# A dynamic convolution with a maxout layer: first chunk in halves with a bit mask for its halo, weights doubled by ScalarE, softmax one chunk ahead of the sums, output copies of two PSUM banks

## The chip, the cores and the metric

The kernel runs on one core of one Trainium2 chip. Times are device microseconds (us) of one execution. "Span" is the time from the first to the last instruction of the profiled execution; it is 1.7 to 2.2 us shorter than the time of that same execution.

## The reference

A causal convolution over 7 rows whose weights are different at each row and for each of 8 groups of 24 columns (a softmax of 7 given numbers), then a layer that takes the larger of two products and projects back.

```python
# x (8, 4160, 192), weight_gen (8, 4160, 8, 7), moe_w1, moe_w2 (192, 1024), moe_w_out (1024, 192)
w = np.exp(weight_gen - max); w = w / (sum(w) + 1e-9)          # over the 7
x_pad = concatenate([zeros(B, 6, D), x], axis=1)               # the halo of each sequence is zero
y[b, s, h, g] = sum over k of w[b, s, h, k] * x_pad[b, s + k, h, g]
h1 = y @ w1; h2 = y @ w2
out = np.maximum(h1, h2) @ w_out
```

## The kernel before

Partition p holds 260 consecutive rows, so 16 partitions hold one sequence. The rows are taken in "chunks" (8, 8, 8, then 14 of 16, then 8 and 4 rows a partition), each chunk in "units" of 8 rows (4 in the first two and the last). VectorE makes the softmax and the convolution of a chunk; a DMA transposes it to `yt`; TensorE makes the hidden layer of a unit while it makes the outputs of the unit before; ScalarE does exp, relu and the output copies. max(h1, h2) is computed as h1 + relu(h2 - h1), so only the difference `wd` of the weights goes through the hidden layer and a small product `w10` gives the first term.

The convolution multiplies 24 columns by one weight. Each weight is stored twice (`[1, 2]`, innermost), so that the multiply reads the weights in pairs. The product e x 1/sum writes both copies itself:

```python
def conv(ci):                                   # VectorE, one chunk; TH = rows * 8 heads, n = rows * 192
    nc.vector.reduce_sum(out=sum_t, in_=_sub(e_t, 0, [[K, TH], [1, K]]), axis=AX.X)
    nc.vector.reciprocal(out=rec_t, in_=sum_t)
    nc.vector.tensor_tensor(                    # "the product": bf16, each weight written twice
        out=_sub(en_t, 0, [[2, TH], [2 * TH, K], [1, 2]]),
        in0=_sub(e_t, 0, [[K, TH], [1, K], [0, 2]]),
        in1=_sub(rec_t, 0, [[1, TH], [0, K], [0, 2]]), op=ALU.mult)
    nc.vector.tensor_tensor(out=m_t, in0=..., in1=..., op=ALU.mult)    # "the multiply": 7 shifted rows of x
    if ci + 2 < len(CHUNKS):
        load(ci + 2)
    # ... three adds, the last into y_t
```

```python
# start: the zero halo of each sequence's first partition is a transfer of its own,
# ahead of the five weight transfers in the same queue
nc.sync.dma_start(out=xb_t[0:P:RPB, 0:PAD * D], in_=zero_t[0:P:RPB, :])
# ... exp(0); conv(0); weight subtractions on VectorE; weight casts on ScalarE; w10 by TensorE
for u in range(NU + 1):
    while queued < NCH and queued <= UNITS[min(u + 3, NU - 1)][0]:
        exp(queued); conv(queued); queued += 1  # exp(1) comes after all weight casts on ScalarE
    if u == 0: transpose(0)
    if u + 1 < NU: transpose(u + 1)             # ahead of unit u's output transfer in the queue
    # ... four quarters: hidden matmuls, relus, output matmuls, one copy of 384 elements per output pair
```

The softmax here doesn't subtract the row's maximum and nothing guards it: scores larger than these inputs give would overflow.

## Time and profile before

| | before |
|---|---|
| time, median of 3 runs | 477.84 us |
| span of the profiled run | 476.3 us |
| TensorE / VectorE / ScalarE busy | 90% / 88% / 71% |
| start of the fifth unit on TensorE | 88.41 us |
| VectorE, one 16-row chunk | 25.6 us |
| TensorE, two units | 25.24 us |

Two views are added. The first is the summary of the chain of waits, which is followed back from the last instruction; it gives each engine's share of the span.

```profile
PE 81%; DVE 11%; DMA 5%; SPq 1%; ACT 1%; issue 0%; POOLq 0%
```

TensorE carries four fifths of it: after the start, TensorE works and the rest keeps up. The second view is VectorE's timeline over one chunk in mid-kernel (start us, duration us, instruction, output<-inputs).

```profile
191.05 11.36 DVE L138 TENSOR_TENSOR m_t<-xb_t,en_t 128x21504 bf16<-128x21504 bf16 x1
...
214.61 2.03 DVE L130 TENSOR_TENSOR en_t<-e_t,rec_t 128x1792 bf16<-128x1792 bf16 x1
216.67 11.36 DVE L138 TENSOR_TENSOR m_t<-xb_t,en_t 128x21504 bf16<-128x21504 bf16 x1
```

From one multiply to the next are 25.62 us, with no gap. VectorE is thus within 0.4 us of TensorE's 25.24: a chunk may grow by nothing on VectorE without the bound moving there.

### The profile page before, as it was taken

To read this page: it belongs to the slowest core of one execution; us is meant where nothing else is said; L and a number is where in the kernel's file an instruction comes from. 1 tells how busy PE (TensorE), PEld (TensorE's weight loads), DVE (VectorE), ACT (ScalarE), POOL (GpSimd) and SP (SyncE) were. 2 spreads that over 40 slices of the span, in tenths; PEclk is the share of its full clock that TensorE was granted. 3 is DMA by queue.
4 is the path that set the end of the run, shared out by engine and by line. 5 is a ranking of instruction groups with operands and counts; after the bars stand their busy time and mean duration, and the time that the engine had idled before them with its cause. 6 is when DMAs were issued, how large, how long until landed. Compare 5 with 4: busy or idle time off the path is not lost.

```text
span 476.3 us, 8155 instructions
## 1 busy us (share of the span) xinstructions
PE 427.1 (90%) x3606; PEld 271.5 (57%) x3606; DVE 418.6 (88%) x136; ACT 336.5 (71%) x437; POOL 22.1 (5%) x46
## 2 busy tenths in 40 slices
PE   0087695599999999999999999989999999999997
PEld 0054353366666666666666666656666666666675
DVE  2949999999999999999999999999999999997000
ACT  1266374287877878787878787867878787777773
POOL 3000000000000000000000000000000000000000
PEclk9999698599999999999999999999999999999999
DMA  8945745546574737467585747384736537273212
GB/s 168 261 107 104 170 120 129 133 93 169 131 175 123 199 107 174 150 139 190 131 200 125 206 85 219 76 192 109 200 109 139 172 67 200 43 200 100 83 67 100
DMA packets 62131, 67.47 MB, mean 142 GB/s; under 512 B 52329, under 2 KB 53609, under 8 KB 60304
## 3 DMA queue, kind: packets, MB, share of 16 engines
q1 hardware_dynamic: 57792, 41.12, 31.1%
q0 software_dynamic: 4304, 25.84, 24.9%
q8 instruction: 28, 0.46, 0.4%
q14 instruction: 7, 0.06, 0.0%
HBM read 46.58 MB, written 25.56 MB: 151 GB/s over the span
## 4 chain that ended last, share of the span: by engine, by line
PE 81%; DVE 11%; DMA 5%; SPq 1%; ACT 1%; issue 0%; POOLq 0%
PE op_ps L292 34%; PE hdp L243 22%; PE hdp L258 13%; PE op_ps L279 7%; DVE m_t L138 5%; PE op_ps L287 4%; DMA wso<-in_moe_w_out_dram 3%; DVE m_t L149 2%; DMA yt<-y_t 2%; DVE m_t L151 1%; DVE en_t L130 1%; PE pw L211 1%; DVE y_t L154 1%; DMA wg_t<-in_weight_gen_dram 1%; DVE sum_t L125 1%; DVE rec_t L127 1%
## 5 line engine op out<-in xcount | busy, mean ns | idle before, releaser
L269 ACT ACTIVATE rd_t<-hdp 128x1024 bf16<-128x1024 f32 (+1 forms) x272 | 267.5, 986 | 112.0 <-PE hdp L258 77.2
L292 PE MATMUL op_ps<-wo,rd_t 128*128 128x192 bf16 x2080 | 216.6, 248 | 0.0
L292 PEld LDWEIGHTS <-rd_t 128*128 128x128 bf16 x2080 | 177.8, 99 | 23.7 <-issue 0.9
L138 DVE TENSOR_TENSOR m_t<-xb_t,en_t 128x21504 bf16<-128x21504 bf16 (+2 forms) x19 | 185.0, 9738 | 5.5 <-DMA xb_t<-zero_t 4.9
L243 PE MATMUL hdp<-yt,wdE 128*128 128x512 bf16 (+1 forms) x272 | 101.6, 374 | 20.8 <-DMA yt<-y_t 18.3
L243 PE MATMUL hdp<-yt,wdO 128*128 128x512 bf16 (+1 forms) x272 | 101.5, 373 | 0.0
L258 PE MATMUL hdp<-yt,wdR 64*128 64x512 bf16 (+1 forms) x544 | 81.6, 375 | 1.1 <-ACT rd_t L269 1.1
L149 DVE TENSOR_TENSOR m_t<-m_t 128x9216 bf16<-128x9216 bf16 (+2 forms) x19 | 81.0, 4263 | 0.7
L303 ACT COPY o_t<-op_ps 128x384 f32<-128x384 f32 x130 | 61.6, 474 | 2.5 <-PE op_ps L292 2.3
L151 DVE TENSOR_TENSOR m_t<-m_t 128x6144 bf16<-128x6144 bf16 (+2 forms) x19 | 55.0, 2894 | 0.7
L258 PEld LDWEIGHTS <-wdR 64*128 64x128 bf16 x544 | 16.2, 94 | 58.1 <-issue 57.5
L279 PE MATMUL op_ps<-w10R,yt 128*128 128x384 bf16 x130 | 44.0, 339 | 0.0
L279 PEld LDWEIGHTS <-yt 128*128 128x128 bf16 x130 | 12.4, 96 | 53.1 <-issue 52.8
L243 PEld LDWEIGHTS <-wdE 128*128 128x128 bf16 x272 | 26.8, 99 | 22.0 <-DMA yt<-y_t 19.6
L287 PEld LDWEIGHTS <-yt 128*128 128x128 bf16 x260 | 25.7, 99 | 14.8 <-issue 0.6
L130 DVE TENSOR_TENSOR en_t<-e_t,rec_t 128x1792 bf16<-128x1792 bf16 (+2 forms) x19 | 33.4, 1755 | 0.7
L287 PE MATMUL op_ps<-w10E,yt 128*128 128x192 bf16 x130 | 32.2, 248 | 0.0
L287 PE MATMUL op_ps<-w10O,yt 128*128 128x192 bf16 x130 | 32.2, 248 | 0.0
L154 DVE TENSOR_TENSOR y_t<-m_t 128x3072 bf16<-128x3072 bf16 (+2 forms) x19 | 29.0, 1527 | 0.7
L243 PEld LDWEIGHTS <-wdO 128*128 128x128 bf16 x272 | 26.8, 99 | 3.6 <-issue 3.4
L125 DVE TENSOR_REDUCE sum_t<-e_t 128x128 f32<-128x896 bf16 (+2 forms) x19 | 17.9, 944 | 9.9 <-ACT e_t L115 9.9
L105 POOL DMA_DIRECT2D xb_t<-in_x_dram x18 | 9.5, 529 | 333.4 <-DVE m_t L138 333.4
(29 smaller groups left out, 69.0 us busy)
## 6 DMA issues: line engine op xcount, KB each, us to landing
out_dram<-o_t SPq DMA_DIRECT2D x31, 768.0 KB, 3.9
xb_t<-in_x_dram POOLq DMA_DIRECT2D x14, 1056.0 KB, 7.8
wg_t<-in_weight_gen_dram POOLq DMA_DIRECT2D x14, 448.0 KB, 6.1
xb_t<-in_x_dram POOLq DMA_DIRECT2D x3, 672.0 KB, 7.9
wg_t<-in_weight_gen_dram POOLq DMA_DIRECT2D x4, 224.0 KB, 5.5
wso<-in_moe_w_out_dram SPq DMA_DIRECT2D x1, 768.0 KB, 13.5
out_dram<-o_t SPq DMA_DIRECT2D x2, 384.0 KB, 3.6
yt<-y_t SPq DMA_TRANSPOSE x34, 3.8
```

Source lines behind the costliest of these rows:

```text
L130: nc.vector.tensor_tensor(out=_sub(en_t, 0, [[2, TH], [2 * TH, K], [1, 2]]), in0=_sub(e_t, 0, [[K, TH], [1, K], [0, 2]]), in1=_sub(rec_t, ...
L138: nc.vector.tensor_tensor(out=m_t, in0=_sub(xb_t, 0, [[D, K], [1, n]]), in1=_sub(en_t, 0, [[2 * TH, K], [2, TH], [0, D // H // 2], [1, 2]] ...
L149: nc.vector.tensor_tensor(out=m_t[:, 0:3 * n], in0=m_t[:, 0:3 * n], in1=m_t[:, 3 * n:6 * n], op=ALU.add)
L151: nc.vector.tensor_tensor(out=rows(m_t, 2, 2, 0), in0=rows(m_t, 2, 2, 0), in1=rows(m_t, 5, 2, 1), op=ALU.add)
L154: nc.vector.tensor_tensor(out=y_t, in0=m_t[:, 0:n], in1=m_t[:, 2 * n:3 * n], op=ALU.add)
L243: nc.tensor.matmul(hd_ts[u, f][:, j * 512:j * 512 + N], lhsT=wd[kind][:, f * P:(f + 1) * P], rhs=_sub(yt_ts[u], 2 * j * P, [[3 * P, n // 2 ...
L258: nc.tensor.matmul(hd_ts[u, f][:, j * 512:j * 512 + N], lhsT=wd["R"][r, f * P:(f + 1) * P], rhs=_sub(yt_ts[u][r, :], P, [[3 * P, n // 2], ...
L269: nc.scalar.activation(out=_sub(rd_ts[u], f * 1024, [[512, 2], [1, N]]), in_=_sub(hd_ts.pop((u, f)), 0, [[512, 2], [1, N]]), func=AF.Relu,)
L279: nc.tensor.matmul(op[:, 0:2 * D], lhsT=yt[:, (3 * i + 1) * P:(3 * i + 2) * P], rhs=w10R, start=True, stop=False, skip_group_check=True,)
L287: nc.tensor.matmul(op[:, sl], lhsT=yt[:, (3 * i + 2 * j) * P:(3 * i + 2 * j + 1) * P], rhs=(w10E, w10O)[j], start=False, stop=False, skip_ ...
L292: nc.tensor.matmul(op[:, sl], lhsT=rd[:, f, j * 512 + i * P:j * 512 + (i + 1) * P], rhs=wo[:, f * D:(f + 1) * D], start=False, stop=(f == ...
L303: nc.scalar.copy(out=o_ts[u][:, 2 * i * D:2 * (i + 1) * D], in_=op_ts.pop((u, i))[:, 0:2 * D])
```

## The change

Its intent: get the first chunk to TensorE sooner (no zero transfer, chunk 0 in two halves), take half the product off VectorE by writing single weights and letting ScalarE double them, put the softmax of the next chunk between a chunk's multiply and its sums so that neither ScalarE nor VectorE waits for it, move the weight subtractions to GpSimd, and copy outputs two banks at a time. The core of the diff:

```diff
+    DIRECT = 2                                   # chunks 0 and 1 are still doubled by VectorE
-            nc.sync.dma_start(out=xb_t[0:P:RPB, 0:PAD * D], in_=zero_t[0:P:RPB, :])
+            halo = xb_t[:, 0:PAD * D].bitcast(I32)
+            nc.vector.tensor_scalar(out=halo, in0=halo, scalar1=msk[:, 0:1], scalar2=None,
+                                    op0=ALU.bitwise_and)
 ... soft(ci): reduce, reciprocal, then
+        pair = 2 if ci < DIRECT else 1
+        for o, To in pieces(ci):                 # two halves in chunk 0, else the chunk
+            N = To * H
 ...
+                en_t = pe_.tile([P, K * N], BF16, name="e1_t", tag="e1")
+            nc.vector.tensor_tensor(
+                out=_sub(en_t, 0, [[pair, N], [pair * N, K], [1, pair]]),
+                in0=_sub(e_t, o * WGC, [[K, N], [1, K], [0, pair]]),
+                in1=_sub(rec_t, o * H, [[1, N], [0, K], [0, pair]]),
+                op=ALU.mult,
+            )
+    def dup(ci):
 ...
+        nc.scalar.copy(out=_sub(en_t, 0, [[2, KTH], [1, 2]]),
+                       in_=_sub(e1_ts.pop(ci), 0, [[1, KTH], [0, 2]]))
 ... start
+        exp(1)
+        for o in (0, 4):
+            mul(0, o)
+            adds(0, o)
+        load(2)
-            nc.vector.tensor_tensor(out=dst, in0=ws[kind, 1], in1=ws[kind, 0], op=ALU.subtract)
+            nc.gpsimd.tensor_tensor(out=dst, in0=ws[kind, 1], in1=ws[kind, 0], op=ALU.subtract)
+        soft(1)
+        mul(1)
+        load(3)
 ... w10R is still cleared by GpSimd further down, now behind load(3)
 ... in the loop over units, ca = the next chunk when unit u ends one
+                if i == 1:
+                    if ca + 1 < NCH:
+                        dup(ca + 1)
+                    adds(ca)
+                    if ca + 1 < NCH:
+                        mul(ca + 1)
+                    if ca + 3 < NCH:
+                        load(ca + 3)
+                if i == 2 and ca + 2 < NCH:
+                    exp(ca + 2)
+                    soft(ca + 2)
+            if i == 3 and u + 1 < NU:
+                transpose(u + 1)
 ... output copies
-        nc.scalar.copy(out=o_ts[u][:, 2 * i * D:2 * (i + 1) * D],
-                       in_=op_ts.pop((u, i))[:, 0:2 * D])
+        nc.scalar.copy(out=_sub(o_ts[u], 4 * g * D, [[2 * D, 2], [1, 2 * D]]),
+                       in_=_sub(op_ts.pop((u, g)), 0, [[512, 2], [1, 2 * D]]))
```

## The prediction

> **What bounds the kernel now.** I read the page first (busy shares, slices, groups), then the chain of waits, the timeline of each engine in the first 95 us, a table of windows, and one unit in mid-kernel. A "unit" is 8 rows per partition of hidden and output matmuls; a "chunk" is one or two units prepared together by VectorE (softmax, seven products, adds).
>
> Costliest groups of the page (line, engine, output<-inputs, count | busy us, mean ns | idle before):
>
> ```profile
> L269 ACT ACTIVATE rd_t<-hdp 128x1024 bf16<-128x1024 f32 (+1 forms) x272 | 267.5, 986 | 112.0 <-PE hdp L258 77.2
> L292 PE MATMUL op_ps<-wo,rd_t 128*128 128x192 bf16 x2080 | 216.6, 248 | 0.0
> L138 DVE TENSOR_TENSOR m_t<-xb_t,en_t 128x21504 bf16<-128x21504 bf16 (+2 forms) x19 | 185.0, 9738 | 5.5 <-DMA xb_t<-zero_t 4.9
> L303 ACT COPY o_t<-op_ps 128x384 f32<-128x384 f32 x130 | 61.6, 474 | 2.5 <-PE op_ps L292 2.3
> L130 DVE TENSOR_TENSOR en_t<-e_t,rec_t 128x1792 bf16<-128x1792 bf16 (+2 forms) x19 | 33.4, 1755 | 0.7
> ```
>
> TensorE is busy 90%, VectorE 88%, so the question is who holds whom, and when. The timeline answers it. VectorE and TensorE in the ramp (start us, duration us, instruction, idle before):
>
> ```profile
> 12.01 5.76 DVE L138 TENSOR_TENSOR m_t<-xb_t,en_t 128x10752 bf16<-128x10752 bf16 x1 [4.86 <-DMA xb_t<-zero_t]
> 31.98 0.62 DVE L125 TENSOR_REDUCE sum_t<-e_t 128x64 f32<-128x448 bf16 x1 [6.58 <-ACT e_t L115]
> ...
> 82.76 1.76 DVE L154 TENSOR_TENSOR y_t<-m_t 128x3072 bf16<-128x3072 bf16 x1
> 88.41 0.61 PE L243 MATMUL hdp<-yt,wdE 128*128 128x512 bf16 x1 [10.34 <-DMA yt<-y_t]
> ```
>
> Up to 88.4 us the end is set by VectorE: it waits 4.86 us for the halo's zero transfer and 6.58 us for an exp queued behind the weight preparation on ScalarE, then runs without a gap until the first 16-row chunk is out at 84.5; a transpose of 3.8 us follows, and TensorE has stood 10.34 us. After that TensorE sets the end. The table of windows (PE, weight load, VectorE, ScalarE, GpSimd busy us, clock, DMA share, GB/s):
>
> ```profile
> 119.65:132.27 12.62, 12.62 (x110) 8.02 (x109) 12.55 (x3) 10.39 (x14) 1.07 (x2) 1.00 0.59 145
> 301.00:401.00 100.00, 98.24 (x843) 62.38 (x841) 99.17 (x29) 78.08 (x98) 4.28 (x8) 1.00 0.59 146
> ```
>
> A unit is 12.62 us of unbroken TensorE. From 88.4 to the end only one stall is left, the 1.8 us of the second row: VectorE needs 25.61 us a chunk (84.44 to 110.05), TensorE 2 x 12.62 = 25.24, so VectorE falls behind by 0.37 us a chunk. So time = start of the fifth unit + 388 us. Last, the margin of ScalarE in mid-kernel:
>
> ```profile
> 123.77 1.02 ACT L269 ACTIVATE rd_t<-hdp 128x1024 bf16<-128x1024 f32 x1 [0.48 <-PE hdp L258]
> 124.69 0.47 ACT L303 COPY o_t<-op_ps 128x384 f32<-128x384 f32 x1
> 125.42 1.02 ACT L269 ACTIVATE rd_t<-hdp 128x1024 bf16<-128x1024 f32 x1 [0.26 <-PE hdp L243]
> ```
>
> ScalarE is idle only 0.48 + 0.26 us in each quarter of a unit (3.155 us). There are two hidden PSUM buffers, and TensorE's next use of the odd one comes 0.3 us after the relu that frees it (relu from 122.26 to 123.28, matmul at about 123.6). That is the whole slack.
>
> [...]
>
> **The change part by part.**
>
> *Start.* The zero transfer goes; a bit mask on VectorE[...] takes its place. The five weight transfers no longer queue behind it: they are issued from about 1.6 us, not 6.87, so they share the DMA with chunk 0's x. In the kernel before the DMA is 90% busy from 3 to 21 us, so this mostly reorders. Chunk 0's main transfer landed about 9.3 us (issue 2.46 + 6.8); shared with weights I put the first multiply at t0 = 10.5, a gain of 1.5.
>
> *VectorE up to the first multiply of chunk 1's end.* Two halves at 5.93 each (the last chunk's 4-row form, 432.29 to 438.22) = 11.9; softmax of chunk 1, 2.37; its multiply, 5.8. Sum 20.05. The two weight subtractions (1.22 + 1.21) leave VectorE[...]. So chunk 1's multiply ends at m1 = 10.5 + 20.05 + 3.0 = 33.55.
>
> *New wait 1.* The order of GpSimd's instructions puts the memset of w10R behind the loads of chunk 3, and those wait for chunk 1's multiply. ScalarE copies into w10R after it, and exp of chunk 2 and TensorE's first unit stand behind those copies: m1 + 0.55 (issue) + 0.44 (memset) + 0.7 (copies) + some 0.25 of semaphores = m1 + 1.95 = 35.5, where TensorE began at 31.40. Exp adds 0.5: softmax of chunk 2 at m1 + 2.45. With 1.87 for it and 5.26 for chunk 1's adds VectorE is free at m1 + 9.6.
>
> *New wait 2.* Chunk 2's multiply needs doubled weights, which ScalarE makes after the fourth relu of TensorE's second unit. In the kernel before that relu ended 10.8 us after TensorE's start, 0.94 of it an exp that has moved[...]. So 1.95 + 9.8 + 0.75 + 0.95 (copy of 896) = m1 + 13.5: 3.9 us of VectorE idle.
>
> *Then* without a gap: multiply 5.8, softmax of chunk 3 at 2.1 + 1.08 = 3.2 (its product halves from 2.03 to about 1.08), adds 5.26, multiply 11.4, softmax of chunk 4 (now ahead of the adds) 3.2, adds 10.1: 39.0. Chunk 3 is out at m1 + 52.5, and with 3.9 for the transpose the fifth unit starts at m1 + 56.4 = 90.0, against 88.41. What the start and the hidden exp win is spent on the two new waits, the lock, and softmax of chunk 4.
>
> *Mid-kernel.* VectorE saves 1.0 us a chunk: 24.6, below TensorE's 25.24, so the 1.8 us stall goes. ScalarE gains one doubling copy of 1792 a chunk, [...]1.59 net, and its paired output copies of 768 take about 0.8 for two of 0.47. The sum fits (about 21 of 25.2 us), but not the place: after the fourth relu come the copy 1.59, relu 0.92, output copy 0.77, relu 1.02, so the sixth relu ends 4.3 us after the fourth, which ends at 126.34 on the scale above: 130.64. TensorE wants that buffer at 123.60 + 2 x 3.155 = 129.91. It stalls about 0.75 us, once in each of the 12 chunks with a full copy from the fifth unit on: 9.0 us.
>
> *End.* One output copy and one larger transfer: +0.4.
>
> *Sum.* 90.0 + 387.9 - 1.8 + 9.0 + 0.4 = 485.5 span, + 1.5 (477.84 against the span of 476.3) = 487.0. The lock and the stall are the least supported and can only be smaller if the engines interleave kindly; counted at 80% they take off 2.4: **484.5 us**.
>
> **Rivals.** (a) The change does what it intends: x lands at 8.5 us, no lock, no stall. Even so VectorE has 66 us of work from there to chunk 3's output, so the fifth unit can't start before 79, and with the two waits 84: 84 + 386 + 1.5 = 472, or 466 without them. Against: the instruction order shows both waits. (b) ScalarE's copies hold TensorE more, a relu late in each later quarter too: 1.2 us a chunk, 492. Against: by the sum above ScalarE catches up by the eighth relu. (c) The doubling copy gates VectorE so late that each chunk waits for its transpose: copy done 8.3 us into a unit, + 24.75 + 3.8 to 5.5 = 37 to 38.6, needed at 38.7. Just enough; if it fails, 1 us a chunk more, 497.
>
> **Range and chances.** t0 is uncertain by 1.5, the lock by 1.5, the waits by 2, the stall by 4 in sum; roughly 5 in all, and more on the low side, since I may overrate the stall. 473 to 493. Faster by 2% means under 468.3, which needs rival (a) nearly whole: 0.06. Slower by 2% means over 487.4: 0.35. The rest, 0.59, is within.
>
> **What would show it.** In the changed kernel: VectorE's first multiply near 10.5; gaps on VectorE ahead of chunk 2's softmax (for ScalarE's exp) and multiply (for the doubling copy); TensorE's first hidden matmul near 35.5; its fifth unit near 90; in mid-kernel one idle of about 0.75 us on the 64-row matmuls every second unit, released by a relu; GpSimd's subtractions with VectorE gaps beside them. The prediction is wrong if the fifth unit starts before 82 or if the mid-kernel has no such idle.

The forecast came to **484.5 us** (487.0 less 2.4). The 3.0 in m1, which the text calls the lock, is an allowance for GpSimd's subtractions holding VectorE up. The 0.75 in "New wait 2" is an allowance for a slow start of TensorE. Both are guesses, worked out from no trace; without the two the sum would be 3.75 lower. The 1.59 for the doubling copy: the kernel before gives nearly the same; ScalarE takes 0.47 us for 384 elements and 1.02 for 1024, so 0.86 ns for each further element; that makes an estimated 1.68 us for 1792 elements, less about 0.10 by which one instruction overlaps the next there (123.77 + 1.02 against 124.69), and 0.80 for an output copy of 768. The changed kernel's took 1.68 and 0.80 us. The 0.25 "of semaphores" is a guess as well; in the kernel before 0.29 us pass from the end of a multiply (17.77) to the load that waits for it (18.06).

## The result, and the profile after

The changed kernel takes **517.0 us** (median of 4 runs, 515.78 to 517.93) where the kernel before took 477.76 in the same rounds: a ratio of 1.081, 95% interval 1.078 to 1.085. Ratios here are the mean time of one kernel's fast runs over the mean of the other's fast runs of the same rounds, so not quite the ratio of the medians. The span of the profiled run is 514.5 us at a mean granted clock of 0.966 (before: 0.975). The prediction, 484.5 in 473 to 493, was wrong.

The summary of the chain of waits of the changed kernel:

```profile
DVE 64%; PE 22%; ACT 3%; DMA 2%; issue 0%; SPq 0%; DVEq 0%; ACTq 0%
```

The bound has moved from TensorE (81% before) to VectorE. The costliest groups of the page say with what (line, engine, output<-inputs, count | busy us, mean ns of one | idle before):

```profile
L147 DVE TENSOR_TENSOR e_t<-e_t,rec_t 128x896 bf16<-128x896 bf16 (+2 forms) x17 | 63.6, 3741 | 0.6
...
L350 ACT COPY o_t<-op_ps 128x768 f32<-128x768 f32 x65 | 51.7, 795 | 2.7 <-PE op_ps L338 2.5
...
L160 ACT COPY en_t<-e_t 128x1792 bf16<-128x1792 bf16 (+2 forms) x17 | 25.9, 1524 | 0.0
```

The product (now L147) was to be halved; its group went from 33.4 us (19 of them, L130) to 63.6 us (17 of them) with half the elements. The output copies fell from 61.6 to 51.7 us, and the new doubling copies cost ScalarE 25.9. VectorE's timeline over one chunk, to set beside the one shown before:

```profile
179.39 11.36 DVE L170 TENSOR_TENSOR m_t<-xb_t,en_t 128x21504 bf16<-128x21504 bf16 x1
...
192.77 4.15 DVE L147 TENSOR_TENSOR e_t<-e_t,rec_t 128x896 bf16<-128x896 bf16 x1
...
206.97 11.36 DVE L170 TENSOR_TENSOR m_t<-xb_t,en_t 128x21504 bf16<-128x21504 bf16 x1
```

From multiply to multiply are 27.58 us, not 24.6, and the difference is nearly all in the 4.15 us of the product. TensorE, which needs 25.24, now waits in each chunk. Its timeline shows it (idle before, and its releaser, in brackets), and so does the table of windows (PE, weight load, VectorE, ScalarE, GpSimd busy us, clock, DMA share, GB/s):

```profile
206.70 0.39 PE L303 MATMUL hdp<-yt,wdR 64*128 64x512 bf16 x2 [0.57 <-ACT rd_t L314]
210.64 0.39 PE L288 MATMUL hdp<-yt,wdE 128*128 128x512 bf16 x1 [1.36 <-DMA yt<-y_t]
```

```profile
301.00:401.00 100.00, 95.67 (x796) 60.17 (x794) 99.08 (x29) 77.83 (x83) 4.32 (x8) 0.98 0.58 142
```

The 0.57 is the stall on ScalarE that the prediction expected (0.75). The 1.36 behind it is new: TensorE waits for the transpose of what VectorE has finished too late. Over these 100 us TensorE is busy 95.67 where it was 98.24.

In the ramp, VectorE first, then GpSimd, then TensorE:

```profile
11.05 0.52 DVE L111 TENSOR_SCALAR xb_t<-xb_t,msk 128x576 int32<-128x576 int32 x1 [9.71 <-DMA xb_t<-in_x_dram]
...
13.80 2.95 DVE L170 TENSOR_TENSOR m_t<-xb_t,en_t 128x5376 bf16<-128x5376 bf16 x1
...
24.15 2.98 DVE L187 TENSOR_TENSOR m_t<-m_t 128x1536 bf16<-128x1536 bf16 x1
27.16 2.58 DVE L191 TENSOR_TENSOR y_t<-m_t 128x768 bf16<-128x768 bf16 x1
...
40.36 0.62 DVE L135 TENSOR_REDUCE sum_t<-e_t 128x64 f32<-128x448 bf16 x1 [2.58 <-ACT e_t L124]
...
51.70 5.76 DVE L170 TENSOR_TENSOR m_t<-xb_t,en_t 128x10752 bf16<-128x10752 bf16 x1 [2.77 <-ACT en_t L160]
```

```profile
23.56 2.76 POOL L229 TENSOR_TENSOR wdE<-ws1E,ws0E 128x1024 bf16<-128x1024 f32 x1
26.28 3.04 POOL L229 TENSOR_TENSOR wdR<-ws1T,ws0T 64x1024 bf16<-64x1024 f32 x1
...
38.61 0.44 POOL L251 MEMSET w10R<- 128x384 bf16 x1
```

```profile
39.78 0.37 PE L288 MATMUL hdp<-yt,wdE 128*128 128x256 bf16 x1 [11.32 <-ACT w10R L261]
...
100.31 0.61 PE L288 MATMUL hdp<-yt,wdE 128*128 128x512 bf16 x1 [6.07 <-DMA yt<-y_t]
```

VectorE waits until 11.05 us for the halo. The softmax of chunk 0, which the kernel before had done by 7.14, now stands behind the mask and ends at 13.80, so the first multiply is later than before (13.80 against 12.01). Two adds of 0.96 and 0.56 us take 2.98 and 2.58 while GpSimd subtracts. TensorE begins at 39.78 (before: 31.40), for want of `w10R`, whose clearing GpSimd reached at 38.61. The fifth unit starts at 100.31, 11.9 us later than before. From there to the end are 414.2 us, where it was 387.9. So of the 38.2 us of span lost, 11.9 were lost in the ramp (up to the fifth unit) and 26.3 after it.

### The profile page after: what moved, and what is told of

Read it like the earlier page. It is cut to its first block, busy times and chain, and to the rows that moved or that the text cites. A ratio compares the mean times of both kernels' runs of the same rounds, so it can differ in the third digit from the quotient of the medians.

```text
span 514.5 us, 8098 instructions
## 1 busy us (share of the span) xinstructions
PE 439.6 (85%) x3606; PEld 276.7 (54%) x3606; DVE 450.7 (88%) x141; ACT 351.1 (68%) x389; POOL 28.6 (6%) x49
## 4 chain that ended last, share of the span: by engine, by line
DVE 64%; PE 22%; ACT 3%; DMA 2%; issue 0%; SPq 0%; DVEq 0%; ACTq 0%
DVE m_t L170 26%; DVE m_t L185 11%; DVE e_t L147 10%; PE op_ps L338 9%; DVE m_t L187 8%; PE hdp L288 6%; DVE y_t L191 4%; PE hdp L303 4%; DVE sum_t L135 2%; DMA yt<-y_t 2%; DVE rec_t L137 2%; PE op_ps L325 2%; ACT rd_t L314 1%; PE op_ps L333 1%; ACT en_t L160 1%
## 5 line engine op out<-in xcount | busy, mean ns | idle before, releaser
L338 PE MATMUL op_ps<-wo,rd_t 128*128 128x192 bf16 x2080 | 219.2, 250 | 0.0
L338 PEld LDWEIGHTS <-rd_t 128*128 128x128 bf16 x2080 | 180.1, 100 | 24.5 <-issue 1.7
L288 PE MATMUL hdp<-yt,wdO 128*128 128x512 bf16 (+1 forms) x272 | 103.5, 380 | 0.0
L303 PE MATMUL hdp<-yt,wdR 64*128 64x512 bf16 (+1 forms) x544 | 85.5, 383 | 7.6 <-ACT rd_t L314 7.6
L185 DVE TENSOR_TENSOR m_t<-m_t 128x9216 bf16<-128x9216 bf16 (+2 forms) x20 | 84.7, 4233 | 0.1
L147 DVE TENSOR_TENSOR e_t<-e_t,rec_t 128x896 bf16<-128x896 bf16 (+2 forms) x17 | 63.6, 3741 | 0.6
L187 DVE TENSOR_TENSOR m_t<-m_t 128x6144 bf16<-128x6144 bf16 (+2 forms) x20 | 57.2, 2859 | 0.7
L350 ACT COPY o_t<-op_ps 128x768 f32<-128x768 f32 x65 | 51.7, 795 | 2.7 <-PE op_ps L338 2.5
L191 DVE TENSOR_TENSOR y_t<-m_t 128x3072 bf16<-128x3072 bf16 (+2 forms) x20 | 31.2, 1559 | 0.7
L160 ACT COPY en_t<-e_t 128x1792 bf16<-128x1792 bf16 (+2 forms) x17 | 25.9, 1524 | 0.0
```

The lines of the kernel that those rows point to most:

```text
L147: nc.vector.tensor_tensor(out=_sub(en_t, 0, [[pair, N], [pair * N, K], [1, pair]]), in0=_sub(e_t, o * WGC, [[K, N], [1, K], [0, pair]]), i ...
L185: nc.vector.tensor_tensor(out=m_t[:, 0:3 * n], in0=m_t[:, 0:3 * n], in1=m_t[:, 3 * n:6 * n], op=ALU.add)
L187: nc.vector.tensor_tensor(out=rows(0, 2, 2), in0=rows(0, 2, 2), in1=rows(1, 5, 2), op=ALU.add)
L191: nc.vector.tensor_tensor(out=y_ts[ci][:, o * D:o * D + n], in0=m_t[:, 0:n], in1=m_t[:, 2 * n:3 * n], op=ALU.add)
L288: nc.tensor.matmul(hd_ts[u, f][:, j * 512:j * 512 + N], lhsT=wd[kind][:, f * P:(f + 1) * P], rhs=_sub(yt_ts[u], 2 * j * P, [[3 * P, n // 2 ...
L303: nc.tensor.matmul(hd_ts[u, f][:, j * 512:j * 512 + N], lhsT=wd["R"][r, f * P:(f + 1) * P], rhs=_sub(yt_ts[u][r, :], P, [[3 * P, n // 2], ...
```

## The experiments

Theory A: the product is slow because of how it writes (single 2-byte elements that each hop), and this alone makes VectorE the bound. Rival B: the doubling as a whole (the copies on ScalarE and the waits for them) costs the time, and the product's length is a side effect. Rival C: the ramp is the larger loss, and mid-kernel would have followed it anyway. All kernels gave correct results. Times are medians; each batch has its own runs of the kernel before (477.22, 478.17, 477.58 and 476.85 us).

### What makes the product slow

**e1_f32**: the changed kernel with 4-byte elements in the product's output.

```diff
-                en_t = pe_.tile([P, K * N], BF16, name="e1_t", tag="e1")
+                en_t = pe_.tile([P, K * N], FP32, name="e1_t", tag="e1")
```

> One edit to the changed kernel: the softmax product of the later chunks is kept in fp32, so VectorE's writes hop as before but are 4 bytes each, not 2. Theory A (the 2-byte hopping write costs 4.15 us where some 1.08 was predicted, and VectorE's 27.6 us a chunk is the whole mid-kernel loss): the product falls to 1.5 to 2.3 us, the chunk to 25.0 to 25.8 us, the time to 488 to 496 us. Theory B (ScalarE's copy and the new order gate VectorE, so the period stays): period 27.5 us with idle on VectorE, time above 510. Theory C (the operands read, not the write, are slow): the product stays near 4.15, time 515 to 518.

**e2_loop**: the changed kernel, product walked in the order of its output, so that it writes without hops and reads with them.

```diff
-                out=_sub(en_t, 0, [[pair, N], [pair * N, K], [1, pair]]),
-                in0=_sub(e_t, o * WGC, [[K, N], [1, K], [0, pair]]),
-                in1=_sub(rec_t, o * H, [[1, N], [0, K], [0, pair]]),
+                out=_sub(en_t, 0, [[N, K], [1, N]]),              # for pair == 1 only
+                in0=_sub(e_t, o * WGC, [[1, K], [K, N]]),
+                in1=_sub(rec_t, o * H, [[0, K], [1, N]]),
```

> One edit to the changed kernel: the same product into the same layout, but looped in the order of the output, so writes are contiguous and the bf16 input hops by 14 bytes. Theory A (hopping 2-byte writes cost): product about 1.1 us, up to 2 if hopping reads cost as well; chunk under 25.5, then TensorE with its stall of 0.57 us on ScalarE sets 25.8; time 484 to 490. Theory B (gating): 510 or more. Theory C (reading these operands is slow): product 4 us or more, 515 to 518.

**e3_actperm**: the changed kernel, product without hops on either side; ScalarE's doubling copy puts the weights in order.

```diff
+                out=_sub(en_t, 0, [[K, N], [1, K]]),              # for pair == 1 only
+                in0=_sub(e_t, o * WGC, [[K, N], [1, K]]),
+                in1=_sub(rec_t, o * H, [[1, N], [0, K]]),
 ...
-        nc.scalar.copy(out=_sub(en_t, 0, [[2, KTH], [1, 2]]),
-                       in_=_sub(e1_ts.pop(ci), 0, [[1, KTH], [0, 2]]))
+        nc.scalar.copy(out=_sub(en_t, 0, [[2 * N, K], [2, N], [1, 2]]),
+                       in_=_sub(e1_ts.pop(ci), 0, [[1, K], [K, N], [0, 2]]))
```

> One edit to the changed kernel: the product is written contiguously in the input's order, and ScalarE's doubling copy reads with a hop of 14 bytes, so it permutes as well. Theory A: product 1.0 to 1.1 us, time 484 to 490 if ScalarE's hopping read is free, more if the copy is longer than 1.68 us. Theory B: above 510. Theory C: product near 4 us.

**l3_slot**, run later: the changed kernel, still single 2-byte elements, but each in a 4-byte word of its own, so that no word is written twice.

```diff
-                out=_sub(en_t, 0, [[pair, N], [pair * N, K], [1, pair]]),
+                out=_sub(en_t, 0, [[2, N], [2 * N, K], [1, pair]]),
 ...
-                       in_=_sub(e1_ts.pop(ci), 0, [[1, KTH], [0, 2]]))
+                       in_=_sub(e1_ts.pop(ci), 0, [[2, KTH], [0, 2]]))
```

> The changed kernel; the single product still writes 2-byte elements, but each into a 4-byte slot of its own, so no two elements of it share a word (hops are 256 bytes as with 4-byte elements). If the 4.15 us come from the element's size, the product stays at 4.1 to 4.2 us and the time at 515 to 519. If they come from neighbours sharing one 4-byte word that is written twice, the product falls to 1.6 to 1.8 us and the time to 493 to 497.

Measured: 494.46, 494.53, 495.62 and 515.71 us. The product's group in the changed kernel and in these four, in the order named (form of 896 elements alone; the third number from the right is the mean in ns):

```profile
L147 DVE TENSOR_TENSOR e_t<-e_t,rec_t 128x896 bf16<-128x896 bf16 x14 | 58.1, 4150 | 0.5
```

```profile
L147 DVE TENSOR_TENSOR e_t<-e_t,rec_t 128x896 f32<-128x896 bf16 x14 | 24.0, 1716 | 0.5
```

```profile
L155 DVE TENSOR_TENSOR e_t<-e_t,rec_t 128x896 bf16<-128x896 bf16 x14 | 22.3, 1590 | 0.5
```

```profile
L155 DVE TENSOR_TENSOR e_t<-e_t,rec_t 128x896 bf16<-128x896 bf16 x14 | 15.3, 1091 | 0.5
```

```profile
L147 DVE TENSOR_TENSOR e_t<-e_t,rec_t 128x896 bf16<-128x896 bf16 x14 | 58.0, 4143 | 0.5
```

For these 896 elements hopping writes of 2 bytes took 4.15 us, of 4 bytes 1.72; the same 2-byte elements written in a row took 1.59, or 1.09 if nothing hops. Sharing a 4-byte word with a neighbour has no part in it: with a word for each element the product took 4.14. The length of the hop has none that shows either, as the forms of 448 and 224 elements, with hops a half and a quarter as long, took 2.16 and 1.16, and l3_slot's hop is twice as long as the changed kernel's (512 bytes for 256; its expectation names the wrong one). Three different repairs of this one instruction each give back 21 to 23 us, so theory A holds for that part. The times of e2_loop and e3_actperm nevertheless missed their expectation (484 to 490): the product fell as expected, but the ramp wasn't counted, where the fifth unit still starts at 98.62 and 96.57 (88.41 before). In e1_f32 the fifth unit starts at 97.83 (2.5 earlier) and the rest takes 394.4 us, 19.8 less than in the changed kernel. Some 17 us against the kernel before were left, so A isn't the whole. Rival C doesn't fit: the ramp holds the smaller part of the loss, and mid-kernel recovered 19.8 us while the fifth unit moved by 2.5.

### Is it the doubling as such?

**e4_direct**: the changed kernel with no doubling on ScalarE at all.

```diff
-    DIRECT = 2
+    DIRECT = 99
```

> One edit to the changed kernel: no doubling by ScalarE at all, the product is written twice by VectorE as before (2.03 us, 4 bytes at a time). Theory A: VectorE 25.6 us a chunk as in the kernel before, no stall of TensorE on ScalarE, no wait for the copy; what is left against the kernel before is the ramp: 478 to 486. Theory B: the same here, since it blames the copy; so this run tells what the doubling cost in all, not why.

Measured: 495.43 us; the expected 478 to 486 was missed. The product is back at 2.03 us for 1792 elements, and ScalarE stalls TensorE no longer. But VectorE is back at 25.5 us a chunk, more than TensorE's 25.24, now waits 11.7 us in all for exps, and the transposes come late (TensorE idle 11.98 before its third unit and 9.62 before its fourth). The fifth unit:

```profile
102.62 0.38 PE L288 MATMUL hdp<-yt,wdE 128*128 128x512 bf16 x1
```

That is 4.8 us later than in e1_f32, and the rest takes 492.1 - 102.62 = 389.5 us, 4.9 less than in e1_f32 and near the 387.9 of the kernel before. Why the transposes of the ramp come so late in e4_direct wasn't followed up. So doubling on ScalarE with a sound product (494.46) and no doubling (495.43) cost the same here, for different reasons. The kernels that keep the doubling and mend the product gain as much as the one without doubling, so rival B doesn't explain these 21 to 23 us. What the copy itself costs is the question of k2_split, below.

### What the ramp costs

Each of the next four adds one edit to e1_f32.

**g1_memset**: clearing `w10R` ahead of the load that made it wait.

```diff
+        nc.gpsimd.memset(w10R, 0.0)        # before load(2)
...
-        nc.gpsimd.memset(w10R, 0.0)        # after load(3)
```

> Base: the changed kernel with the fp32 product (e1_f32, 494.5 us, fifth unit at 97.8). One more edit: GpSimd's memset of w10R moved ahead of the loads of chunk 2. If the memset behind the loads is what holds ScalarE's copies, chunk 2's exp and TensorE's start (39.75): TensorE starts at 31 to 34, VectorE's waits of 2.6 us (exp) and 4.0 us (doubling copy) shrink to under 2 in all, the fifth unit starts at 88 to 92, time 484 to 489. If the late start is set by something else (weight transfers, the doubled weights), the waits stay and the time is 493 to 495.

**g2_subdve**: the weight subtractions back on VectorE.

```diff
-            nc.gpsimd.tensor_tensor(out=dst, in0=ws[kind, 1], in1=ws[kind, 0], op=ALU.subtract)
+            nc.vector.tensor_tensor(out=dst, in0=ws[kind, 1], in1=ws[kind, 0], op=ALU.subtract)
```

> Base e1_f32. One more edit: the two weight subtractions go back to VectorE. If GpSimd's reads lock VectorE out (two adds took 2.98 and 2.58 us instead of 0.96 and 0.56, 4.04 us in all): those adds fall to 0.96 and 0.56, VectorE gets 2.43 us of subtractions back, a net gain of 1.6 us on the path; 492 to 494. If the long adds have another cause, they stay long and the time is 496 to 498.

**g3_tearly**: transposes issued half a unit earlier.

```diff
-            if i == 3 and u + 1 < NU:
+            if i == 1 and u + 1 < NU:
                 transpose(u + 1)
```

> Base e1_f32. One more edit: each transpose is issued in the second quarter of the unit before, not at its end, so it no longer stands behind an output transfer that waits for a paired copy. If that order is what makes TensorE stand 5.65 us before its third unit and 6.05 us before its fourth: these fall to under 2 us each, the doubling copy of chunk 3 comes earlier, VectorE's wait of 2.7 us goes, the fifth unit starts at 94 to 96, time 491 to 493. If VectorE alone sets the ramp, the third and fourth unit move and the fifth does not: 494 to 496.

**k1_wlast**: a tiny transfer out of x ahead of the weights in the same queue, so that they are issued once x has landed.

```diff
+        scr = pstage.tile([1, 16], BF16, name="scr")
+        nc.sync.dma_start(out=scr, in_=xb_ts[0][0:1, PAD * D:PAD * D + 16])
```

> Base e1_f32 (494.5 us, first multiply at 13.76, fifth unit at 97.8). One more edit: the five weight transfers are issued only when chunk 0's x has landed (a tiny transfer out of x goes ahead of them on the same queue). If the weights' place in the DMA is what made x land at 11 to 13.7 us: the first multiply starts at 9 to 10.5, VectorE gains 3 to 4 us unless it then waits for the weights' subtraction, the fifth unit starts at 94 to 95, time 490 to 492. If x lands late for another reason (the memset and iota ahead of its issue on GpSimd), the multiply stays after 12.5 and the time at 494.

Measured: 489.35, 493.19, 491.82 and 489.62 us, so 5.1, 1.3, 2.6 and 4.8 us less than e1_f32. g2_subdve and g3_tearly fell into their expected ranges; g1_memset ended 0.35 us above its range and k1_wlast 0.4 below. The 1.3 us of g2_subdve alone are not clear of noise (ratios 1.032 and 1.037 with overlapping intervals); for it the trace speaks. The line that answers for each, in that order: TensorE's first hidden matmul, the first of the two blocked adds, TensorE's third unit, VectorE's first multiply.

```profile
34.81 0.37 PE L288 MATMUL hdp<-yt,wdE 128*128 128x256 bf16 x1 [6.54 <-DMA yt<-y_t]
```

```profile
24.67 0.96 DVE L187 TENSOR_TENSOR m_t<-m_t 128x1536 bf16<-128x1536 bf16 x1
```

```profile
54.13 0.38 PE L288 MATMUL hdp<-yt,wdE 128*128 128x512 bf16 x1 [0.40 <-ACT rd_t L314]
```

```profile
8.87 2.95 DVE L170 TENSOR_TENSOR m_t<-xb_t,en_t 128x5376 bf16<-128x5376 bf16 x1
```

The late memset held both TensorE's start (39.78 in the changed kernel) and ScalarE's exp. Without GpSimd's subtractions the add takes 0.96 us again instead of 2.98, so it was GpSimd that blocked it. In the changed kernel a transpose is issued at the end of a unit, in the queue behind an output transfer. There the queue issued that output transfer at 55.09 and the transpose for the third unit at 55.55, so the unit started at 59.71, though VectorE had made its data by 48.93; in e1_f32 it started at 59.65, in g3_tearly at 54.13. And the first multiply was late by 4.9 us because the weights were moved first. That shows in the list of DMA issues of the first 30 us (output<-input, queue, count, KB each, us from issue to landing), the 384 KB being chunk 0's rows, in the changed kernel and then in k1_wlast:

```profile
xb_t<-in_x_dram POOLq DMA_DIRECT2D x1, 384.0 KB, 10.5
```

```profile
xb_t<-in_x_dram POOLq DMA_DIRECT2D x1, 384.0 KB, 5.3
```

### What the doubling costs in mid-kernel

**k2_split**: e1_f32 with the doubling copy cut in three, in ScalarE's idle places.

```diff
-    def dup(ci):
+    def dup(ci, q0, q1):               # quarters q0 to q1 of the copy
...
+                if i == 0 and ca + 1 < NCH:
+                    dup(ca + 1, 0, 1)
...
+                if ca is not None and i == 1 and ca + 1 < NCH:
+                    dup(ca + 1, 1, 3)
...
-                        dup(ca + 1)
+                        dup(ca + 1, 3, 4)
```

> Base e1_f32. One more edit: the doubling copy is cut in three (a quarter after the second relu, a half ahead of the fourth, a quarter after it), so that each piece falls into idle time of ScalarE. If the place and not the amount of ScalarE's work makes TensorE stand 0.57 us a chunk: that idle goes in all 12 full chunks, 6.8 us less, 487 to 489. If ScalarE is simply too full, the idle stays: 494 or more.

Measured: 485.84 us, 8.6 less, where 6.8 were expected. The table of windows for e1_f32 and then for k2_split (columns as above):

```profile
110.00:210.00 100.00, 97.71 (x833) 62.38 (x831) 95.73 (x26) 80.94 (x85) 3.35 (x7) 1.00 0.61 150
```

```profile
110.00:210.00 100.00, 100.00 (x859) 64.42 (x860) 98.95 (x28) 83.95 (x96) 4.32 (x8) 1.00 0.65 154
```

TensorE goes from 97.71 to 100.00 of 100 us: the stall is the place of the copy and not the amount of ScalarE's work, which is no smaller in the second line. The stall also costs more than the 0.57 us of idle that the timeline lists: in e1_f32 successive ones lie 25.99 us apart (at 226.78 and 252.77, say), 0.75 more than the 25.24 of two units.

### Parts of the change put into the kernel before

**h1_exp**: the kernel before with exp of chunk 1 ahead of the weight casts.

```diff
         exp(0)
+        exp(1)
         conv(0)
...
-            exp(queued)
+            if queued > 1:
+                exp(queued)
```

> The kernel before with one part of the change alone: chunk 1's exp is issued ahead of the weight preparation on ScalarE. By my reading of the kernel before VectorE's ramp sets the end and its idle of 6.58 us is on the path: the fifth unit starts at 81 to 83 instead of 88.4, time 470 to 473. If TensorE's start or the transfers hold the ramp instead: 476 to 478.

**h2_mask**: h1_exp with the bit mask for the halo, chunk 0's `wg_t` in the other queue, and the weights behind x as in k1_wlast (cut: the mask itself and the clearing of partition 0's halo).

```diff
-            nc.sync.dma_start(out=xb_t[0:P:RPB, 0:PAD * D], in_=zero_t[0:P:RPB, :])
+            halo = xb_t[:, 0:PAD * D].bitcast(I32)
+            nc.vector.tensor_scalar(out=halo, in0=halo, scalar1=msk[:, 0:1], scalar2=None,
+                                    op0=ALU.bitwise_and)
...
+        scr = pstage.tile([1, 16], BF16, name="scr")
+        nc.sync.dma_start(out=scr, in_=xb_ts[0][0:1, PAD * D:PAD * D + 16])
```

> On h1_exp (kernel before with the early exp, 472.2 us, first multiply at 12.41): the halo by bit mask instead of a zero transfer, chunk 0's weights by the sync queue, and the five weight transfers behind x as in k1_wlast. If the mask as such is worth what it intends: the first multiply starts at 9 to 10, the fifth unit at 79 to 80, time 469 to 470.5. If the ramp then waits for the weights (they land later): no gain, 472.

**h3_bank2**: the kernel before with the copies of two banks and nothing else (the part of the change's diff headed "output copies").

> The kernel before with the 2-bank output copies alone. My theory: no effect in mid-kernel, since ScalarE is not the bound there, and 0.3 to 0.5 us more at the end; 477.5 to 479. A rival says the paired copies hold TensorE or the transposes: 482 or more.

Measured: 472.2 us (ratio 0.989, 0.986 to 0.991), 469.98 us (0.985, 0.982 to 0.988) and 478.18 us (1.002, 0.999 to 1.004). The fifth unit of h1_exp, then VectorE's first multiply and the fifth unit of h2_mask:

```profile
82.13 0.61 PE L244 MATMUL hdp<-yt,wdE 128*128 128x512 bf16 x1 [8.36 <-DMA yt<-y_t]
```

```profile
8.81 5.76 DVE L144 TENSOR_TENSOR m_t<-xb_t,en_t 128x10752 bf16<-128x10752 bf16 x1
...
78.94 0.61 PE L252 MATMUL hdp<-yt,wdE 128*128 128x512 bf16 x1 [5.86 <-DMA yt<-y_t]
```

The 6.58 us wait for an exp that the prediction read in the kernel before was real time: moving one instruction starts the fifth unit 6.3 us earlier. With mask and order of transfers together, the first multiply starts 3.6 us earlier than in h1_exp (12.41 there) and the fifth unit 3.2; in the time this is some 2 us, and the intervals of the two ratios overlap a little. In the changed kernel, where the weights go first, the mask brought no earlier start (13.80 against 12.01). The order of transfers without the mask wasn't run, so what the mask itself adds isn't shown. Copies of two banks are worth nothing: the 10 us that ScalarE saves are not on the path.

### Is anything unnamed left?

**l1_fixed**: the changed kernel with the product of e3_actperm, g1_memset, g2_subdve, g3_tearly, and the doubling copy in three pieces (weights k = 0 and 1, 2 to 4, 5 and 6).

> The changed kernel with five repairs at once: contiguous product, w10R memset early, weight subtractions on VectorE, transposes one half unit earlier, doubling copy cut into pieces. If the causes named by the single experiments are the whole loss, the fifth unit starts at 84 to 88 us, no stall of TensorE is left in mid-kernel, and the time is 472 to 477, at or below the kernel before. The rival, that these gains overlap (each lifts the same wait) or that something unnamed is left: fifth unit at 90 or later, time 480 to 486.

**l2_fixed**: l1_fixed with k1_wlast's transfer, chunks 2 and 3 doubled by VectorE, and exp of chunk 2 earlier.

```diff
-    DIRECT = 2
+    DIRECT = 4
...
+        exp(2)                              # ahead of the four w10 copies
...
-    exp(2)
     soft(2)
```

> The former with the weights issued behind x, chunks 2 and 3 doubled by VectorE, and exp of chunk 2 ahead of the last weight copies. First multiply at 8.7 to 9.0 us, no wait for a doubling copy before chunk 4. If the ramp is then bound by VectorE's work alone, fifth unit at 79 to 83 and 467 to 472, level with the best kernel so far (469.98, made from the kernel before). The rival, that transposes, now behind output transfers, hold it: fifth unit at 84 or later, 473 to 477.

Measured: 474.7 us (ratio 0.9947, 0.992 to 0.997) and 469.37 us (0.984, 0.982 to 0.986). Two successive multiplies of l1_fixed on VectorE, then the fifth unit of l1_fixed and of l2_fixed:

```profile
57.90 11.36 DVE L180 TENSOR_TENSOR m_t<-xb_t,en_t 128x21504 bf16<-128x21504 bf16 x1
...
82.51 11.36 DVE L180 TENSOR_TENSOR m_t<-xb_t,en_t 128x21504 bf16<-128x21504 bf16 x1
```

```profile
86.18 0.61 PE L298 MATMUL hdp<-yt,wdE 128*128 128x512 bf16 x1 [3.70 <-DMA yt<-y_t]
```

```profile
81.93 0.61 PE L301 MATMUL hdp<-yt,wdE 128*128 128x512 bf16 x1 [3.04 <-DMA yt<-y_t]
```

After the fifth unit neither of the two lists any wait of TensorE. The single gains over e1_f32 (g1 5.1, g2 1.3, g3 2.6, k2 8.6) sum to 17.6, and together, with e3_actperm's shorter product, they give 19.8 (474.7 from 494.46, in two batches whose runs of the kernel before differ by 0.4). So there is no sign that they overlap, and they cover the loss against the kernel before. They don't cover all: l1_fixed also has the early exp, and h1_exp, with the early exp alone, takes 472.2 us and starts its fifth unit 4.05 us earlier (82.13). Part of that is by design, since l1_fixed makes the softmax of the next chunk (3.1 us, from 69.17 to 72.28) ahead of the sums that the fifth unit waits for; no run isolates it. l2_fixed and h2_mask come from the two kernels by different ways and cannot be told apart in time (0.984 and 0.985 with overlapping intervals). Both beat the kernel before by about 1.5%, with intervals below 1.

| kernel | us | ratio to before | fifth unit at |
|---|---|---|---|
| before | 477.8 | 1 | 88.41 |
| changed | 517.0 | 1.081 | 100.31 |
| l3_slot (2-byte hops, own words) | 515.71 | 1.081 | 100.56 |
| e1_f32 (4-byte hops) | 494.46 | 1.037 | 97.83 |
| e2_loop (no hop on writes) | 494.53 | 1.037 | 98.62 |
| e3_actperm (no hop) | 495.62 | 1.039 | 96.57 |
| e4_direct (no doubling) | 495.43 | 1.039 | 102.62 |
| e1_f32 + g2_subdve | 493.19 | 1.032 | 96.59 |
| e1_f32 + g3_tearly | 491.82 | 1.030 | 94.98 |
| e1_f32 + k1_wlast | 489.62 | 1.025 | 92.74 |
| e1_f32 + g1_memset | 489.35 | 1.025 | 92.63 |
| e1_f32 + k2_split | 485.84 | 1.019 | 97.99 |
| l1_fixed | 474.7 | 0.995 | 86.18 |
| l2_fixed | 469.37 | 0.984 | 81.93 |
| before + h1_exp | 472.2 | 0.989 | 82.13 |
| before + h2_mask | 469.98 | 0.985 | 78.94 |
| before + h3_bank2 | 478.18 | 1.002 | 86.88 |

## Why the prediction was wrong

**The step that failed** is "its product halves from 2.03 to about 1.08", and with it "VectorE saves 1.0 us a chunk: 24.6, below TensorE's 25.24". The product took 4.15 us. The mechanism the prediction reasoned with (halve the elements, halve the time) took a duration from a row with other access: 1.08 is the time of a product that writes pairs of adjacent elements, and the new one writes single 2-byte elements that hop. VectorE rose from 25.6 to 27.58 us a chunk instead of falling to 24.6, and became the bound. With the writes mended, l1_fixed needs 82.51 - 57.90 = 24.61 us, just the number of the prediction.

The product isn't the whole miss. e3_actperm has the product at the predicted length (1.09 us), and the prediction's sum holds from the fifth unit to the end: 492.0 - 96.57 = 395.4 us, where its terms give 387.9 - 1.8 + 9.0 + 0.4 = 395.5. But its fifth unit starts 6.6 us later than the predicted 90.0, and its 495.62 us lie outside the range as well. In it the start was 3.0 us late, the lock took 1.0 more than predicted, and a wait that wasn't foreseen took 2.98 (all three below); they sum to 7.0 of these 6.6.

The kernel before could not have given the time: all 19 of its products (L130) write pairs. The runs give it per element, fixed part included: 1716 / 896 = 1.9 ns where e1_f32 writes single 4-byte elements that hop, 4150 / 896 = 4.6 ns where the changed kernel writes single 2-byte ones, and 1091 / 896 = 1.2 ns where e3_actperm writes them without a hop.

Point by point:

- **Start at 10.5**: wrong, 13.80. "This mostly reorders" was right in kind, but the order was the wrong way: the weights went ahead of x. k1_wlast, with x first, starts at 8.87. That the softmax of chunk 0 would stand behind the mask (0.52 us) was overlooked.
- **The lock, 3.0 us**: an allowance without support in the trace before; it came true, a little small. The two adds grew by 2.98 - 0.96 and 2.58 - 0.56, 4.0 in all, while GpSimd subtracted for 2.76 and 3.04 us; g2_subdve, where VectorE subtracts (1.22 and 1.21 us), removes it.
- **Chunk 1's multiply ends at 33.55**: 37.78, the two errors above summed (3.3 + 1.0).
- **New wait 1, 2.45 us behind the multiply**: right, 2.58; g1_memset shows its cause.
- **New wait 2, 3.9 us**: there, 2.77 in the changed kernel and 4.01 in e1_f32. The close agreement is partly luck: 10.8 us after TensorE's start is where the fifth relu ended in the kernel before, not the fourth (about 10.25), and in e1_f32 the fourth ended some 11.1 us after it.
- **Fifth unit at 90.0**: 100.31. The start is 3.3 of this, the lock 1.0, and three products instead of the assumed ones (2.16 for 0.62, twice 4.15 for 1.08) 7.7; the shorter second wait takes 1.1 back. That sums to 10.9 of the 10.3 found. Mending the product alone brings only 2.5 of the 7.7 back, because waits take its place, the second wait above and the next point.
- **"*Then* without a gap"**: wrong once the product is mended. Chunk 3's multiply waits 2.72 us for its doubling copy in e1_f32 (0.26 in the changed kernel, where the slow product fills the time), because TensorE's third unit is late. In g3_tearly the wait is gone.
- **The stall of TensorE on ScalarE, 0.75 in each of 12 chunks**: right, in place and size: 0.57 of listed idle, 0.75 in the period of e1_f32, in 12 chunks. In the changed kernel it stands in the trace too (0.57), but VectorE's 27.58 us a chunk set the period; that it costs nothing there was not tested. With the product mended it counts: from the fifth unit to the end e1_f32 takes 394.4 us. k2_split takes it away and the same stretch needs 483.3 - 98.0 = 385.3.
- **The end, +0.4**: a guess, not measured by itself. From the fifth unit to the end h3_bank2 takes 475.8 - 86.88 = 388.9 us, where the kernel before took 387.9, in one profile of each; the timed runs tell no difference.
- **Rival (a)**, the intended gain, needed x at 8.5 and no lock; both are to be had, but only in another order. **Rival (c)**, chunks that wait for their transpose, is what the changed kernel does, but by VectorE's length and not by a late copy.
- **Not foreseen at all**: the transposes, now behind output transfers in one queue, left TensorE idle 5.68 us before its third unit; 2.6 us of the time, by g3_tearly.
- **Slips in the working that change little**: 126.34 is where the next instruction can follow the fourth relu, which itself ends at 126.44 (125.42 + 1.02 in the line shown); 487.0 - 2.4 is 484.6. The discount to 80% rested on the lock and the stall being smaller; the lock was larger (4.0) and the stall as computed. The 0.75 for a slow start of TensorE was no more than a guess. What the trace of the kernel before shows of such a start is at the fifth unit, after 10.34 us of idle: the granted clock was 0.50 from 88.41 to 94.00, and the first shorter matmul (0.42 us for 0.63) came at 94.37, some 6.0 us after the start.

The 0.35 given to "slower by 2%" came true by a step that the prediction did not have. The range failed because the prediction counted its uncertainty only in terms that it had called uncertain. The product's 1.08 was treated as a fact; none of the rivals let VectorE become slower.

## What to carry to other kernels

Halving the elements of an instruction need not halve its time if the access changes (2.03 us became 4.15 here): look for a row with the same element size and the same steps, and if there is none, give the term a range of its own. Where two engines are within 0.4 us of each other per round, as VectorE and TensorE here, ask of every edit what it does to both. When a change loses, mending its parts one at a time shows what each was worth; here one of them (an exp ahead of the weight casts) made the kernel before 1.1% faster by itself, and with x ahead of the weights and a mask for the halo it came to 1.5%.
